# Attention with a learned distance bias and a two-layer FFN: weights' low bits on ScalarE, more first-layer rows on VectorE, new ranks for the early work

## The chip, the cores and the metric

The kernel runs on one core of one Trainium2 chip. The metric is the device time of one execution in microseconds; before the change the median of three runs is 672.18 us (670.63 to 674.49). A core has TensorE (PE; matmuls, with the loading of weights beside it, PEld), VectorE (DVE), ScalarE (ACT), GpSimd (POOL) and SyncE (SP), which here only issues DMAs. Each engine works through its own queue in order; a wait holds everything behind it on that engine.

## The reference

Attention over 4 batches, 8 heads, 576 positions and a head dimension of 64, with a bias that a small network makes from the distance of two positions, and then a feed-forward block over all 2304 tokens. All inputs are 32-bit floats except the two FFN weights, which are 64-bit floats.

```python
scores = scale * np.matmul(q, k.transpose(0, 1, 3, 2))
rel = (pos[:, None] - pos[None, :]).astype(np.float32)
x = (np.log1p(np.abs(rel)) / np.log1p(np.maximum(pos[:, None], 1.0)))[..., None]
bias = np.maximum(x @ w1 + b1, 0.0) @ w2        # 32 hidden units, 8 heads
scores = scores + bias.transpose(2, 0, 1)[None]
attn = softmax(scores);  attn_out = attn @ v
h = attn_out_tokens @ w_in                      # 512 -> 2048
g = h * np.clip(h + 3.0, 0.0, 6.0) / 6.0
out = g @ w_out                                 # 2048 -> 512
```

## The kernel before

**Bias tables.** The bias depends on the batch in nothing, so it is made once, in 36 groups of 16 query rows each. `z_group` (L854 to 871) makes the first layer: four tiles of [128, up to 576] for each group, each a maximum of a distance table `T` against a column (on VectorE, L865) or a Relu with a bias column (on ScalarE, L869). Which engine makes which of the four is read from a pattern of letters by `zeng`: A is ScalarE, D is VectorE; `z0` holds for groups 0 to 11, `z1` for 12 to 15, `zeng` for 16 to 35 (far groups, of which only the distances up to the farthest are made). `bias_mm` and `bias_far` multiply with `w2_sb` on TensorE (L907, L886) into one of three two-bank PSUM tiles, `bias_out` empties them on ScalarE (L925), and `bias_store` sends the block to DRAM (L939, on ScalarE's DMA queue). A correction column `cv_sb` for each distinct pattern is copied at the start (L1105). `load_bias` brings tables back from DRAM tile by tile (L500, on SyncE's queue), after all rows that the tile needs were stored.

**Attention.** 144 tiles of 128 query rows. For each: QK on TensorE (L536 is a warm-up product, L539 and L559 the scores), sum with the bias and row maximum on VectorE (L571), exponent on ScalarE (L582). The first 32 tiles (batches 0 and 1, first half of the rows) are `direct`: transposed on TensorE (L634), brought to SBUF on ScalarE (L637), multiplied with V in 32-bit (L675, L686). The others are split into a high and a low 16-bit part (L129 on ScalarE, L146 on VectorE) and transposed by DMA (L654).

**Weights.** `w_in` and `w_out` come as 64-bit floats, in eight pieces of 1 MB each (128 rows of 1024 numbers), and are read as pairs of 32-bit words. `f64_load` (L248) loads a piece, w_in into one of two buffers `w`, w_out into parts of the `wo` and `z_e` tiles. `f64_abs` takes the high word: ScalarE writes its absolute value, scaled, as a 32-bit float (L258), and GpSimd multiplies the high word by zero in place, which leaves its sign bit (L259). `f64_pack` then makes the 32-bit float on VectorE in three passes: clamp with a row maximum (L266), shift left by three and OR the sign (L269), and OR the three top bits of the low word (L272). A row's power-of-two scale follows, and `split_w` makes the high 16-bit part (L129) and the low one (L146): mode A does them on ScalarE and VectorE, mode R scales in place on GpSimd (L134), takes the high part on ScalarE and the low one on GpSimd (L139). `wm1` and `wm2` are the modes for the eight pieces of each weight. `w_in` is staged in `wo`, so w_out's loads into `wo` wait until w_in is split.

**FFN.** `ffn` is a generator with a step for each of 16 slices of hidden units (12 matmuls, L790, then L780, L773, L767, L769) and for parts of the output (L813, L823). Its first run is opened at tile 21 (`START`), when w_in is ready; w_out must be ready before its second layer. `open_steady` at tile 37 writes what is left of it, and from there TensorE's order is fixed as written.

**What sets the order.** The kernel is written as one long program; a scheduler gives every instruction a rank in the order of writing, simulates time, and lets each engine take the ready instruction of lowest rank. `ahead(k)` writes what is in its block with a rank k lower; `low(gen, key)` writes a generator's steps with a rank higher by the configured number (1000 for both weights). Pacing numbers say how many steps of each generator are written for each tile: `rw1` for w_in, `rf0` for the first FFN, `rf` for later ones. `behind(k)` makes a load wait at issue for the k-th bias load.

Of the kernel before, what the change touches and what calls it, by code (L numbers as in the profile page):

```python
# [13 lines left out]
U32 = mybir.dt.uint32  # L14
AF = mybir.ActivationFunctionType
# [4 lines left out]
D = 64  # L20
# [7 lines left out]
CQ = 2.0 ** -25  # L28
VC = 5 * 128
CFG = {'z0': 'AD', 'gz': 12, 'z1': 'AD', 'gz2': 16, 'zeng': 'DDA', 'sg': 'P', 'wm1': 'A', 'wm2': 'RRAAAAAA', 'hl': 'A', 'gl': 'PP', 'vm': 'A', 'g0': 8, 'rwi': 2.0, 'rw0': 0.3, 'rw1': 0.7, 'ro': 0.85, 'rb': 1.7, 'rf0': 1.3, 'rf': 2.0, 'rf1': 1.55, 'la': 6, 'gq': 2, 'gap': 0.0, 'wu': 8, 'act': 'o', 'g1': 2, 'w64': 5, 'rfo': 2.3, 'tv': 'A', 'pw': 1000, 'po': 1000, 'gr': 'AD', 'wb': 3, 'fb': 2, 'spn': 45, 'sw': 37, 'ws': 2, 'kn': 10, 'kw': 1, 'os': 10, 'ro2': 2.0, 'bo': 12, 'rb0': 1.5, 'psw': 21, 'xp': 0, 'mw': 2, 'he': 0}  # L30
# [5 lines left out]
def attention_moe_kernel(  # L36
# [214 lines left out]
    def f64_abs(t, u):  # L251
        if len(t.shape) == 3:
            tv, u = t.rearrange("p a (c w) -> p a c w", w=2), u.rearrange("p (a c) -> p a c", a=2)
            lo, hi = tv[:, :, :, 0], tv[:, :, :, 1].bitcast(F32)
        else:
            tv = t.rearrange("p (c w) -> p c w", w=2)
            lo, hi = tv[:, :, 0], tv[:, :, 1].bitcast(F32)
        nc.scalar.activation(out=u, in_=hi, func=AF.Abs, scale=F64_BIAS)  # L258
        nc.gpsimd.tensor_scalar(  # L259
            out=hi, in0=hi, scalar1=0.0, scalar2=1.0, op0=ALU.mult, op1=ALU.mult  # L260
        )
        return lo, hi.bitcast(U32), u

    def f64_pack(lo, sign, u, top, first=0.0):
        ub = u.bitcast(U32)
        nc.vector.tensor_scalar(  # L266
            out=u, in0=u, scalar1=F64_MAX, scalar2=first, op0=ALU.min, op1=ALU.max, accum_out=top,
        )
        nc.vector.scalar_tensor_tensor(  # L269
            out=ub, in0=ub, scalar=3, in1=sign, op0=ALU.logical_shift_left, op1=ALU.bitwise_or  # L270
        )
        nc.vector.scalar_tensor_tensor(  # L272
            out=ub, in0=lo, scalar=29, in1=ub, op0=ALU.logical_shift_right, op1=ALU.bitwise_or
        )
# [9 lines left out]
    def w_in_prep():  # L284
# [15 lines left out]
        def sign(k, t):  # L300
            c, fs = at(k)
            return f64_abs(t, stage[:, c, fs])
# [26 lines left out]
    def w_out_prep():  # L329
# [19 lines left out]
        def sign(k, t):  # L349
            if k % 2:  # L350
                u = const.tile([128, 2 * S], F32, tag="kb1", name="cu")
            else:
                u = pools["e"].tile([128, 2 * S], F32, tag="cu", name="cu")
            u = u[:, 0:1024]
            return (*f64_abs(t, u), u)
# [672 lines left out]
    def aux(n):  # L1028
# [25 lines left out]
        if b + 1 < B and t < 4 and p >= 1:  # L1054
            if b + 1 not in vgen:
                vgen[b + 1] = v_scale(b + 1)
# [18 lines left out]
    nc.sync.dma_start(out=bp, in_=psi)  # L1075
# [4 lines left out]
    nc.vector.memset(cv_sb, 0.0)  # L1080
# [18 lines left out]
    for k in range(4):  # L1099
        nc.tensor.matmul(out=cps[32 * k:32 * k + 32, 0:1], lhsT=w2_sb, rhs=b1_sb)  # L1100
    for c, pat in enumerate(pats):
        for k in range(4):
            if pat[k]:
# [30 lines left out]

    gen_b = repeat(bias_step)
    gen_w = low(w_in_prep(), "pw")
    gen_v = v_scale(0)
# [5 lines left out]
    HOLD, LAST = 2, NT + 5  # L1143
# [35 lines left out]
    def open_steady():  # L1179
        nonlocal phase  # L1180
        for k in count():
# [3 lines left out]
            if k % 2 and emitted[3] < NG:  # L1185
# [17 lines left out]
    def ffn_step():  # L1203
        nonlocal phase
        taken[0] += 1
        r = next(queue[0], "end")
# [16 lines left out]
    for n in range(-1, NT + 7):  # L1223
# [5 lines left out]
        if n == 12:  # L1229
# [91 lines left out]
```

## Time and profile before

| | before |
|---|---|
| median of three runs | 672.18 us (670.63 to 674.49) |
| the profiled execution | time 673.99 us, span 672.2 us |
| TensorE busy | 634.2 us, 94% of the span |
| weight loads (PEld) | 452.4 us, 67% |
| ScalarE busy | 506.4 us, 75% |
| VectorE busy | 460.0 us, 68% |
| GpSimd busy | 207.6 us, 31% |
| DMA | 130.57 MB, mean 194 GB/s |
| mean granted TensorE clock | 0.977 |

The span runs from the first to the last instruction; the time of an execution is that and what lies around it. A busy share is a mean over stages with different limits. The granted clock is given in parts of TensorE's full speed. A wait names the instruction that stood and the one that came last before it could go.

### The profile page before, as it was taken

How to read it: one execution, taken by the hardware profiler on the slowest of the kernel's cores; microseconds unless marked ns; L12 is line 12 of the kernel's file. 1: busy time of each engine (PE TensorE's matmuls, PEld its weight loads, DVE VectorE, ACT ScalarE, POOL GpSimd, SP SyncE). 2: the span in 40 equal slices, each digit the busy share in tenths (PEclk: the TensorE clock that was granted, in tenths of full speed). 3: DMA queues.
4: the chain of work that ended last, by engine and by line, in shares of the span. 5: the costliest groups of instructions: out<-in, count | busy, mean ns of one | idle time of the engine just before them, and what ended most of it. 6: DMA issues, size and time to landing. Idle time of an engine off the chain costs nothing. (4 is left out here: it accounts for less than half of the span.)

```text
span 672.2 us, 14784 instructions
## 1 busy us (share of the span) xinstructions
PE 634.2 (94%) x5424; PEld 452.4 (67%) x5424; DVE 460.0 (68%) x1114; ACT 506.4 (75%) x1000; POOL 207.6 (31%) x267
## 2 busy tenths in 40 slices
PE   7666799897999999999999999999999999999997
PEld 3223455575676667788888887777777777777775
DVE  6898858999846887677678768776677667720310
ACT  7986677888967998999689879876798669822620
POOL 0212124666111441145034414531245215300420
PEclk9987899898899999999999999999999999999999
DMA  8888966654496999999999999899878986530000
GB/s 293 287 328 310 362 240 236 245 190 166 107 214 187 269 189 237 256 229 208 260 269 253 216 219 202 187 164 184 210 144 167 194 179 124 110 74 20 1 11 29
DMA packets 176648, 130.57 MB, mean 194 GB/s; under 512 B 138304, under 2 KB 145728, under 8 KB 175552
## 3 DMA queue, kind: packets, MB, share of 16 engines
q1 hardware_dynamic: 166784, 114.14, 70.3%
q10 hardware_dynamic: 9792, 15.49, 7.3%
q8 instruction: 42, 0.69, 0.5%
q14 instruction: 30, 0.25, 0.1%
HBM read 77.54 MB, written 15.49 MB: 138 GB/s over the span
## 5 line engine op out<-in xcount | busy, mean ns | idle before, releaser
L790 PE MATMUL h_ps<-x,wi 128*128 128x256 f16 (+1 forms) x1536 | 200.0, 288 | 2.2 <-DVE p_v L161 1.0
L813 PE MATMUL o_ps<-g,wo 128*128 128x256 f16 (+1 forms) x1536 | 196.0, 286 | 0.0
L790 PEld LDWEIGHTS <-wi 128*128 128x128 f16 x1536 | 147.9, 98 | 50.4 <-issue 11.8
L813 PEld LDWEIGHTS <-wo 128*128 128x128 f16 x1536 | 146.9, 98 | 46.9 <-issue 8.8
L769 POOL TENSOR_TENSOR g<-t,g 128x256 f16<-128x256 f32 (+1 forms) x128 | 100.8, 797 | 187.5 <-ACT g L767 186.7
L582 ACT ACTIVATE bt<-bt,sm 128x576 f32<-128x576 f32 x144 | 110.7, 769 | 43.1 <-DVE sm L571 41.4
L146 DVE SCALAR_TENSOR_TENSOR hl<-bt,sm,hl 128x576 f16<-128x576 f32 x112 | 93.9, 851 | 25.5 <-ACT hl L129 22.2
L129 ACT ACTIVATE hl<-bt,sm 128x576 f16<-128x576 f32 x112 | 84.2, 766 | 3.4 <-ACT bt L582 2.3
L773 DVE SCALAR_TENSOR_TENSOR t<-t,t,h_ps 128x320 f32<-128x320 f32 (+1 forms) x112 | 57.0, 515 | 41.7 <-ACT t L780 40.8
L418 POOL TENSOR_TENSOR qkl<-st,qkh 128x576 fp32r<-128x576 f32 (+2 forms) x48 | 54.8, 1163 | 67.7 <-ACT qkh L411 67.0
L767 ACT ACTIVATE g<-t 128x256 f16<-128x256 f32 (+1 forms) x128 | 55.3, 439 | 21.3 <-DVE t L773 21.1
L571 DVE CUSTOM_DVE_ANT_0 bt<-s_ps,bt 128x576 f32<-128x576 f32 x88 | 65.1, 750 | 8.0 <-PE s_ps L559 4.5
L780 ACT ACTIVATE t<-h_ps,t,hr 128x320 f32<-128x320 f32 (+1 forms) x112 | 64.2, 585 | 5.2 <-PE h_ps L790 4.3
L823 ACT ACTIVATE ot<-o_ps,os 128x256 f32<-128x256 f32 (+1 forms) x32 | 15.8, 492 | 45.5 <-PE o_ps L813 45.5
L590 DVE TENSOR_SCALAR sm<-sm 128x1 f32<-128x1 f32 x112 | 16.8, 151 | 40.7 <-ACT bt L582 40.6
L925 ACT ACTIVATE bo<-b_ps,cv_sb,isc 128x576 f32<-128x576 f32 (+36 forms) x60 | 35.9, 640 | 4.0 <-PE b_ps L886 2.1
L865 DVE TENSOR_SCALAR z_e<-T,nbp 128x576 f32<-128x576 f32 (+17 forms) x69 | 31.4, 500 | 7.7 <-PE b_ps L886 6.6
L634 PE MATMUL t_ps<-eye_sb,bt 128*128 128x128 f32 x160 | 26.2, 298 | 10.5 <-DVE sm L571 8.1
L571 DVE CUSTOM_DVE_ANT_0 bt<-s_ps,k 128x576 f32<-128x576 f32 x40 | 28.7, 752 | 9.6 <-PE s_ps L559 7.6
L869 ACT ACTIVATE z_e<-T,bp 128x576 f32<-128x576 f32 (+17 forms) x43 | 29.0, 698 | 8.1 <-PE b_ps L886 4.6
L634 PEld LDWEIGHTS t_ps<-eye_sb,bt 128*128 128x128 f32 x160 | 18.6, 150 | 21.9 <-DVE sm L571 10.7
L721 PE MATMUL pv_ps<-at,vh 128*64 128x320 f16 (+1 forms) x432 | 32.0, 293 | 0.0
(128 smaller groups left out, 835.9 us busy)
## 6 DMA issues: line engine op xcount, KB each, us to landing
bt<-bias SPq DMA_DIRECT2D x36, 576.0 KB, 5.8
w<-in_w_in_dram SPq DMA_DIRECT2D x8, 1024.0 KB, 7.9
vs<-in_vp_dram SPq DMA_DIRECT2D x24, 320.0 KB, 4.8
st<-in_qk_dram SPq DMA_DIRECT2D x16, 448.0 KB, 4.3
bias<-bo ACTq DMA_DIRECT2D x20, 295.5 KB, 5.3
wo<-in_w_out_dram SPq DMA_DIRECT2D x5, 1024.0 KB, 6.2
bias<-bo ACTq DMA_DIRECT2D x16, 288.0 KB, 6.9
bt<-bias SPq DMA_DIRECT2D x32, 144.0 KB, 3.3
```

The lines of the kernel that those rows point to most:

```text
L129: nc.scalar.activation(out=out, in_=full, func=AF.Copy, scale=scale)
L146: nc.vector.scalar_tensor_tensor(out=out, in0=full, scalar=scale, in1=high, op0=ALU.mult, op1=ALU.subtract)
L418: nc.gpsimd.tensor_sub(out=lo[:, c:c + w], in0=t[:, c:c + w], in1=hi[:, c:c + w].bitcast(F32))
L571: nc.vector.tensor_tensor_reduce(out=halves(bt), in0=ps, in1=halves(src), op0=ALU.add, op1=ALU.min, scale=-0.125, scalar=3.0e38, accum_out ...
L582: nc.scalar.activation(out=bt, in_=bt, func=AF.Exp, scale=-1.0, bias=sm[:, 0:1], accum_out=total)
L634: nc.tensor.transpose(tp[:, 128 * c:128 * c + 128], bt[:, j:j + 128], eye_sb)
L767: nc.scalar.activation(out=g[:, 0], in_=uu, func=AF.Copy)
L769: e.tensor_sub(out=g[:, 1], in0=uu, in1=g[:, 0])
L773: nc.vector.scalar_tensor_tensor(out=t_t[f], in0=t_t[f], scalar=cols(f)[2], in1=h_t.pop(f)[:, 0:n], op0=ALU.min, op1=ALU.mult,)
L780: nc.scalar.activation(out=t_t[f], in_=h_t[f][:, 0:n], func=AF.Relu, scale=cols(f)[0], bias=cols(f)[1],)
L790: nc.tensor.matmul(out=h_t[f][:, 0:n], lhsT=wi[:, a, c, f * 128:(f + 1) * 128], rhs=x[:, e, c], start=(k == 0), stop=(k == 3 * KC - 1),)
L813: nc.tensor.matmul(out=ops[:, 0:n], lhsT=wo[:, a, f, e * 128:(e + 1) * 128], rhs=g_t[f][:, r], start=(f == 0 and a == 0 and r == 0), stop= ...
```

## The change

`f64_abs` gets a third step: it reads the low word's upper 16 bits as an unsigned integer, multiplies by 7.499 / 65535 and writes the result, 0 to 7, as a 16-bit integer into the lower half of the high word, which GpSimd has cleared but for the sign. The mode decides on which engine; both weights have mode A, ScalarE, for all pieces. With that the third pass of `f64_pack` is left out, since the OR of the sign brings the three bits along.

The patterns change: `z0` from AD to ADD, `zeng` from DDA to ADDD. `wm1` goes from A for all pieces to R for the first, `wm2` from R for the first two to R for the first. Pacing: `rw1` 0.7 to 0.6, `rf0` 1.3 to 1.6, `rf` 2.0 to 1.95, `wb` 3 to 8. Every function that writes work is wrapped by `ranked`, which moves its rank until the steady part begins; of the new ranks seven are not zero: `a_z` 300, `a_bo` -1000, `a_vl` -15, `a_st` -15, `a_wp` -40, `a_ld` -100, `a_wl` -300. V's scales are wrapped by `low` with 0. The load of psi moves to ScalarE's queue (`s2`). The other new keys (`tn`, `s1`, `il`, `dn`, `v1`, `hold`) have values that leave the code as it was.

```diff
+LOW3 = 7.499 / 65535
...
-'z0': 'AD', 'zeng': 'DDA', 'wm1': 'A', 'wm2': 'RRAAAAAA', 'rw1': 0.7, 'rf0': 1.3, 'rf': 2.0, 'wb': 3
+'z0': 'ADD', 'zeng': 'ADDD', 'wm1': 'RAAAAAAA', 'wm2': 'RAAAAAAA', 'rw1': 0.6, 'rf0': 1.6, 'rf': 1.95, 'wb': 8
+'a_z': 300, 'a_bo': -1000, 'a_vl': -15, 'a_st': -15, 'a_wp': -40, 'a_ld': -100, 'a_wl': -300, 'l31': 'A', 'l32': 'A', 's2': 1
...
-    def f64_abs(t, u):
+    def f64_abs(t, u, mode):
         if len(t.shape) == 3:
...
+            t16 = t.bitcast(U16).rearrange("p a (c w) -> p a c w", w=4)
+            top16, low16 = t16[:, :, :, 1], t16[:, :, :, 2]
...
         nc.scalar.activation(out=u, in_=hi, func=AF.Abs, scale=F64_BIAS)
         nc.gpsimd.tensor_scalar(
             out=hi, in0=hi, scalar1=0.0, scalar2=1.0, op0=ALU.mult, op1=ALU.mult
         )
-        return lo, hi.bitcast(U32), u
+        if mode == "P":
+            nc.gpsimd.tensor_scalar(
+                out=low16, in0=top16, scalar1=LOW3, scalar2=1.0, op0=ALU.mult, op1=ALU.mult
+            )
+        elif mode == "A":
+            nc.scalar.activation(out=low16, in_=top16, func=AF.Copy, scale=LOW3)
+        return lo if mode == "D" else None, hi.bitcast(U32), u
...
         nc.vector.scalar_tensor_tensor(
             out=ub, in0=ub, scalar=3, in1=sign, op0=ALU.logical_shift_left, op1=ALU.bitwise_or
         )
+        if lo is None:
+            return
         nc.vector.scalar_tensor_tensor(
             out=ub, in0=lo, scalar=29, in1=ub, op0=ALU.logical_shift_right, op1=ALU.bitwise_or
         )
...
-    nc.sync.dma_start(out=bp, in_=psi)
+    (nc.scalar if cfg['s2'] else nc.sync).dma_start(out=bp, in_=psi)
...
+    def ranked(f, key):
+        def g(*a):
+            with ahead(0 if steady[0] else cfg[key]):
+                return f(*a)
+        return g
...
+    z_group = ranked(z_group, "a_z")
...
+    bias_out = ranked(bias_out, "a_bo")
+    bias_store = ranked(bias_store, "a_st")
...
+    load_v = ranked(load_v, "a_vl")
+    load_direct = ranked(load_direct, "a_ld")
+    load_qk = ranked(load_qk, "a_ld")
...
+    f64_load = ranked(f64_load, "a_wl")
...
+    f64_pack = ranked(f64_pack, "a_wp")
...
-    gen_v = v_scale(0)
+    gen_v = low(v_scale(0), "a_v")
```

## Rows read from the trace of the kernel before

**Rows 1.** The page's 40 slices, busy tenths of TensorE (a slice is 16.8 us).

```profile
PE   7666799897999999999999999999999999999997
```

**Rows 2.** Busy us by stretch: PE, PEld, DVE, ACT, POOL, granted clock, DMA share, GB/s.

```profile
5.00:34.00 29.00, 21.39 (x207) 9.06 (x206) 23.50 (x53) 27.73 (x39) 4.06 (x3) 1.00 0.89 325
34.00:84.00 50.00, 35.55 (x204) 17.76 (x204) 45.84 (x95) 35.53 (x58) 7.80 (x7) 0.84 0.90 333
84.00:118.00 34.00, 32.23 (x235) 19.43 (x233) 24.69 (x60) 25.72 (x48) 11.68 (x10) 0.98 0.65 240
118.00:168.00 50.00, 43.78 (x329) 30.41 (x327) 47.48 (x100) 42.64 (x83) 31.04 (x29) 0.92 0.56 198
168.00:290.00 122.00, 119.54 (x1120) 86.99 (x1119) 88.13 (x234) 105.36 (x215) 28.24 (x37) 0.98 0.92 212
```

**Rows 3.** Waits between 5 and 50 us: us in total, times, longest.

```profile
PE s_ps L536 <- ACT bo L925: 4.9, 1, 4.9
PE b_ps L907 <- ACT z_a L869: 2.4, 4, 1.3
```

**Rows 4.** The same view between 50 and 84 us, then between 118 and 175 us.

```profile
PE t_ps L634 <- DVE sm L571: 4.9, 3, 2.4
...
PE t_ps L634 <- DVE sm L571: 2.2, 1, 2.2
```

**Rows 5.** Timeline of TensorE, two PV products of one form.

```profile
79.75 4.73 PE L675 MATMUL pv_ps<-atf,vf 128*64 128x256 f32 x20
...
85.98 2.53 PE L675 MATMUL pv_ps<-atf,vf 128*64 128x256 f32 x20
```

**Rows 6.** The same windows of line L272 alone: VectorE busy us and count, clock, DMA.

```profile
5.00:34.00 29.00, 2.43 (x2) 1.00 0.89 325
34.00:84.00 50.00, 7.51 (x6) 0.84 0.90 333
84.00:118.00 34.00, 2.92 (x2) 0.98 0.65 240
118.00:168.00 50.00, 8.51 (x6) 0.92 0.56 198
```

**Rows 7.** Instructions by line and form, 0 to 168 us: busy us, mean ns.

```profile
L146 DVE SCALAR_TENSOR_TENSOR wi<-wo,w1s,wi 128x1024 f16<-128x1024 f32 x8 | 10.1, 1275 | 0.1
L139 POOL TENSOR_TENSOR wo<-cu,wo 128x1024 f16<-128x1024 f32 x2 | 4.7, 2338 | 1.3 <-DMA wo<-in_w_out_dram 1.3
L865 DVE TENSOR_SCALAR z_a<-T,nbp 128x576 f32<-128x576 f32 x16 | 7.6, 512 | 1.5 <-PE b_ps L907 1.5
L129 ACT ACTIVATE wo<-cu 128x1024 f16<-128x1024 f32 x2 | 2.1, 1058 | 2.7 <-POOL cu L134 2.7
```

**Rows 8.** Timeline of ScalarE: start us, us, instruction.

```profile
6.50 1.43 ACT L869 ACTIVATE z_a<-T,bp 128x576 f32<-128x576 f32 x2
...
117.66 1.06 ACT L129 ACTIVATE wo<-cu 128x1024 f16<-128x1024 f32 x1 [2.39 <-POOL cu L134]
118.62 0.55 ACT L780 ACTIVATE t<-h_ps,c,hs 128x256 f32<-128x256 f32 x1
```

**Rows 9.** What SyncE's DMA queue waited for, 0 to 180 us.

```profile
SPq L248 <- DVE wo L272: 32.3, 5, 15.8
SPq L248 <- DVE cu L272: 23.3, 5, 9.3
```

**Rows 10.** The last of these windows for line L869 alone: ScalarE busy us and count.

```profile
168.00:290.00 122.00, 17.13 (x27) 0.98 0.92 212
```

**Rows 11.** Timeline of ScalarE, the first-layer rows at the start.

```profile
5.16 1.44 ACT L869 ACTIVATE z_e<-T,bp 128x576 f32<-128x576 f32 x2 [3.15 <-DVE bp L1089]
```

**Rows 12.** Timeline of ScalarE and TensorE around 37 us.

```profile
32.77 2.17 ACT L129 ACTIVATE wi<-wo,w1s 128x1024 f16<-128x1024 f32 x2
...
37.04 1.15 PE L536 MATMUL s_ps<-T,eye_sb 128*128 128x288 f32 x2 [4.91 <-ACT bo L925]
```

**Rows 13.** Timeline of VectorE, the first attention tile's softmax.

```profile
39.68 0.76 DVE L571 CUSTOM_DVE_ANT_0 bt<-s_ps,bt 128x576 f32<-128x576 f32 x1
```

More of the change, by code (lines that the diff above doesn't have):

```diff
@@ L14 @@
 U32 = mybir.dt.uint32
+U16 = mybir.dt.uint16
 AF = mybir.ActivationFunctionType
@@ L301, in sign @@
             c, fs = at(k)
-            return f64_abs(t, stage[:, c, fs])
+            return f64_abs(t, stage[:, c, fs], pick("l31", k))
         def pack(k, tu):
@@ L354, in sign @@
             u = u[:, 0:1024]
-            return (*f64_abs(t, u), u)
+            return (*f64_abs(t, u, pick("l32", k)), u)
         def pack(k, tu):
@@ L631, in soft_low @@
             tp = s_bank("t_ps").rearrange("p a b -> p (a b)")
+            if n < cfg["tn"]:
+                for _ in range(cfg["tw"]):
+                    nc.tensor.matmul(out=tp[:, 0:128], lhsT=eye_sb, rhs=eye_sb)
             for c in range(5):
@@ L1053, in aux @@
                 split_v_b(*units[k])
-        if b + 1 < B and t < 4 and p >= 1:
+        if b + 1 < B and t < 4 and p >= 1 and n >= cfg["v1"]:
             if b + 1 not in vgen:
-                vgen[b + 1] = v_scale(b + 1)
+                vgen[b + 1] = low(v_scale(b + 1), "a_v")
             next(vgen[b + 1], None)
@@ L1079, in attention_moe_kernel @@
     nc.sync.dma_start(out=T[:, 0:512], in_=ltab[:, 0:512])
-    nc.vector.memset(cv_sb, 0.0)
+    if cfg["s1"]:
+        nc.gpsimd.memset(cv_sb, 0.0)
+        for c, pat in enumerate(pats):
+            for k in range(4):
+                if pat[k]:
+                    nc.gpsimd.memset(cv_sb[32 * k:32 * k + 32, c:c + 1], 1.0)
+    else:
+        nc.vector.memset(cv_sb, 0.0)
     nc.vector.memset(c36[:, 0:1], 3.0 * CQ)
@@ L1100, in attention_moe_kernel @@
         nc.tensor.matmul(out=cps[32 * k:32 * k + 32, 0:1], lhsT=w2_sb, rhs=b1_sb)
+    if cfg["s1"]:
+        nc.vector.tensor_scalar(
+            out=cv_sb, in0=cv_sb, scalar1=cps[:, 0:1], scalar2=None, op0=ALU.mult
+        )
     for c, pat in enumerate(pats):
         for k in range(4):
-            if pat[k]:
+            if pat[k] and not cfg["s1"]:
                 rows = slice(32 * k, 32 * k + 32)
@@ L1142, in attention_moe_kernel @@
     START, SWITCH = 21, cfg["sw"]
-    HOLD, LAST = 2, NT + 5
+    HOLD, LAST = cfg['hold'], NT + 5
     in_order = ctx.enter_context(ExitStack())
@@ L1184, in open_steady @@
             ffn_step()
-            if k % 2 and emitted[3] < NG:
+            if k % cfg['il'] and emitted[3] < NG:
                 bias_step()
@@ L1205, in ffn_step @@
         taken[0] += 1
-        r = next(queue[0], "end")
+        with ahead(0 if steady[0] else cfg["a_ff"]):
+            r = next(queue[0], "end")
         if r == "w2":
@@ L1228, in attention_moe_kernel @@
             next(gen_v, None)
-        if n == 12:
+        if n == cfg["dn"]:
             distances()
```

19 lines of the change are left out of this document (18 added, 1 removed).

## The prediction

> **What bounds the kernel now.** I read the page's 40 slices first [rows 1]. From about the twelfth slice on TensorE is in the highest tenth to the end, with one dip; the room lies in the first ten slices, with 6 to 9 tenths. So nothing that the change does to ScalarE or VectorE late in the span can pay much, and what it does before 168 us pays only where TensorE stands still there. I then cut the early part by what runs in it [rows 2] and subtract TensorE's busy time from each stretch: idle are 29.0 - 21.4 = 7.6 us from 5 to 34 us (call it A), 50.0 - 35.6 = 14.4 us from 34 to 84 us (B), 1.8 us from 84 to 118 us (C), 6.2 us from 118 to 168 us (D), and 2.5 us of the 122 us after that (E). About 30 us are to be had before 168 us, and no more, unless the clock rises too.
>
> Who is full in each stretch differs, and that is what the change must be held against. In A ScalarE works 27.7 of 29.0 us; VectorE 23.5. In B VectorE works 45.8 of 50 us and ScalarE 35.5, while the DMA engines are 0.90 busy. In C nobody is full but TensorE. In D VectorE works 47.5 of 50 us and ScalarE 42.6. In E ScalarE is at 105.4 of 122. The waits say the same: up to 50 us TensorE waits for ScalarE (4.9 us once for a bank that a bias row block had to leave, 2.4 us for first-layer rows) [rows 3]; after that for VectorE's softmax (4.9 us in B, 2.2 us in D) [rows 4]. The granted clock is 0.84 in B and 0.92 in D [rows 2], so between the levels of 1.2 and 2.4 GHz part of the time: one and the same product of 20 matmuls takes 4.73 us just after a thin stretch and 2.53 us a few us later [rows 5].
>
> **Part 1, the low bits.** Sixteen weight pieces (eight of w_in, eight of w_out) lose their last VectorE pass, L272: two in A with 2.4 us, six in B with 7.5, two in C with 2.9, six in D with 8.5, together 21.3 us [rows 6]. In their place ScalarE runs 16 copies of 128x1024, 16-bit in and out, with steps of four elements. No row shows such a copy. The nearest is the 128x1024 copy with a constant scale: 1.06 us long [rows 7], 0.96 us from its start to that of the next instruction [rows 8]. Below, it could not go under what a ScalarE instruction of 1024 elements takes at all here, so 0.96; above I take the slowest mean of the L272 it replaces, 2.92 / 2 = 1.46 us in C [rows 6]. I use 0.96, the row with the same engine, operation and size: 15.4 us in all, up to 23 at the upper end. So 21 us leave VectorE and 15 go to ScalarE.
>
> The Trainium skill, "ScalarE: Activation LUTs", section "Rules for kernel authors", says the opposite of what is done here: a multiplication belongs on VectorE rather than on ScalarE. The rows above have the two passes nearly equal, because the VectorE one reads two 32-bit operands; going by the rule one would book no gain for this part, and the sum below would end near the time of before. That case stands among the rivals.
>
> The pass also sits in a chain: ScalarE's absolute value, GpSimd's clearing of the high word, the new copy, then VectorE's shift-and-or, which until now waited for GpSimd alone. In return the last reader of a w_in buffer, and with it what the next weight load waits for, is no longer L272. SyncE's queue now stands 32.3 us in five waits and 23.3 us in five more for exactly that instruction [rows 9], and everything behind it in that queue (bias and value loads) stands too. One pass leaves that chain and one of about the same length enters: I cost the release at nothing, with one pass of 1 to 1.5 us for each of the three dependent rounds of w_in loads either way as its bounds, so plus or minus 5 us.
>
> **Part 2, first-layer rows.** In the first twelve groups VectorE makes two rows of three instead of one of two: 32 instead of 24, so ScalarE loses 8. Two ScalarE rows take 1.43 us back to back [rows 8], so 8 x 0.72 = 5.7 us less there, and 8 x 0.51 = 4.1 us more on VectorE [rows 7], which has 5.5 us idle in A [rows 2] and loses two L272 there. In the far groups (20, all in E) ScalarE makes 20 rows instead of 27. The 27 take 17.1 us [rows 10], so the 7 some 4.4 us of ScalarE, but TensorE is idle for only 2.5 us of E, and other releasers share that: I take 0.5 us. Three more copies of one column for the additional patterns of rows lie on VectorE at the start, beside its idle time in A.
>
> **Part 3, piece modes.** The first w_in piece gets its low half on GpSimd instead of VectorE (1.28 us less there), the second w_out piece gets it on VectorE instead of GpSimd (1.28 us more, and 2.34 us plus a scaling pass less on GpSimd) [rows 7]. GpSimd is busy for 4.1 of 29 us in A and 7.8 of 50 in B [rows 2], so it hides the first; C has 9.3 us of VectorE idle to hide the second.
>
> **Part 4, ranks, pacing and loads.** The psi load goes to ScalarE's queue, one slot of SyncE earlier for all that follows it. ScalarE's first row waits 3.15 us for the product of that load [rows 11]; one slot is about 0.4 us. The first-layer rows go 300 ranks ahead, the emptying of the bias banks 1000 behind, weight loads 300 and the pack 40 behind, and the third w_out load waits for a later bias load. All of this moves work and adds none. Its price depends on the order that the scheduler writes, which no row shows; it is bounded by the idle time it can fill or open, and I give it -6 to +10 us, and zero in the sum, except that it lets A's relief come through.
>
> **The sum, stretch by stretch.** A: ScalarE, which is full, loses 5.7 us and gains two copies, 1.9 us: -3.8, of which I count 3.5. B: VectorE falls by six L272, 7.5 us, and one low half of 1.28, from 45.8 to 37.0 us; ScalarE rises by 5.8 to 41.3. The fuller of the two falls by 4.5 us; transfers limit part of this stretch (0.90 busy), so I count 3. C: 0. D: VectorE falls by six L272, 8.5 us, to 39.0; ScalarE rises by 5.8 to 48.4 of 50, above the 47.5 that VectorE had. The fuller engine has 0.9 us more: +1. E: -0.5. Start: -0.4. Together -3.5 - 3 + 1 - 0.5 - 0.4 = -6.4 us. The span of the profiled execution is 672.2 us, its own time 673.99, the median of three runs 672.18; the difference of span and time is 1.8 us and stays, and the median is 1.8 us below the profiled execution. So I take 672.2 - 6.4, near **666 us** for the median.
>
> **Rivals.**
> *ScalarE becomes what VectorE was.* For: over A to D the busier engine has 23.5 + 45.8 + 24.7 + 47.5 = 141.5 us (VectorE) now, and afterwards 27.7 + 35.5 + 25.7 + 42.6 = 131.5 plus 15.4 minus 5.7 = 141.2 us (ScalarE). If a queue that full is what makes tiles late, whichever engine it is, nothing is won; only start and E remain, and the time is 671 us, with 669 to 675 about it. Against: B and A have different full engines, and the change relieves each in its place. This is also where the rule of the Trainium skill above would lead.
>
> *Late bank emptying, slower.* L925, which empties the bias banks, loses 1000 ranks, while the weight passes on the same in-order queue, now one more for each piece, do not. The pattern is in the trace: two weight copies hold ScalarE for 2.17 us from 32.77 us on, and TensorE's next score matmul, at 37.04, has waited 4.91 us for an emptying behind them [rows 12]. Several w_in pieces are worked on while the 16 near groups run. If two or three more of them cut in like that, at up to 4.9 us each, the tables and with them all softmaxes come 10 to 15 us later, and A's relief of 3.5 is gone: 672 + 10 to 15 - 3 = 679 to 684, say 680 us. It decides from the point where the eighth group's store lands later than now, since the first tile's bias load waits for it. Against: rows cannot run far ahead, as only two groups' buffers and three banks exist.
>
> *More than the sum.* The early gap of B closes further, the clock stays up (2.2 us for one product alone [rows 5]), and tiles start earlier by all of A: up to half of the 30 us idle, 655 us. It is the far end of the forecast, not a case of its own.
>
> **How the numbers follow.** A measurement of this kernel can tell about 0.5%, 3.4 us, from no change. Forecast with its far end (655 to 668.5 us): 0.58. ScalarE in VectorE's place (669 to 675): 0.22. Late emptying or another order that stalls (over 675.5): 0.20. The likeliest case's own range is 657 to 669. To leave out no more than 2 in 10, the range goes from 655 to 679: it cuts off gains of over half the idle time and the far half of the slower case, and takes in the copy's upper price (16 x 0.5 = 8 us of ScalarE) and the bounds of the release.
>
> **What would show it.** Right: no L272; a 16-bit ScalarE copy near 1.0 us at 16 places; VectorE under 40 of 50 us in B; the first softmax before 39.68 us [rows 13]; SyncE's waits for L272 replaced by shorter ones; the start of TensorE's full stretch some 6 us earlier. Wrong: the copy at 1.5 us or more; first softmax after 40 us with TensorE waiting for L925; ScalarE over 48 of 50 us from B on with the softmax exponent late; or a full stretch that begins earlier and a tail that gives it back.

## The result and the profile after

| | before | after |
|---|---|---|
| median | 671.96 us (4 runs, 670.63 to 674.49) | 679.27 us (4 runs, 678.25 to 680.08) |
| ratio | | 1.0103, 95% interval 1.007 to 1.0136 |
| the profiled execution | 673.99 us, span 672.2 | 678.25 us, span 676.4 |
| TensorE busy; rest of the span | 634.2; 38.0 us | 633.5; 42.9 us |
| ScalarE busy, VectorE busy | 506.4, 460.0 us | 531.9, 452.1 us |

The change made the kernel 7.3 us slower, where 6.2 us faster was forecast. TensorE's busy time is nearly the same; the span holds 4.9 us more in which it does nothing. First, busy time by stretch after the change, with the columns and stretches of [rows 2]:

```profile
5.00:34.00 29.00, 22.06 (x207) 10.54 (x206) 24.08 (x60) 27.14 (x33) 5.94 (x4) 0.88 0.84 304
34.00:84.00 50.00, 34.95 (x206) 17.11 (x208) 40.34 (x83) 47.11 (x62) 8.67 (x7) 0.83 0.86 308
84.00:118.00 34.00, 28.42 (x189) 15.90 (x189) 21.52 (x65) 29.10 (x48) 8.69 (x8) 0.90 0.66 238
118.00:168.00 50.00, 43.90 (x333) 30.81 (x330) 40.06 (x92) 48.67 (x76) 24.16 (x24) 0.93 0.59 218
168.00:290.00 122.00, 117.89 (x1109) 84.84 (x1110) 94.25 (x236) 104.42 (x215) 30.99 (x41) 0.99 0.86 208
```

The fuller engine has changed sides. From 34 to 84 us ScalarE now works 47.1 of 50 us (35.5 before) and VectorE 40.3 (45.8); from 118 to 168 us ScalarE is at 48.7. From 84 to 118 us, where nobody but TensorE had been full, TensorE lost 3.8 us of work (32.2 to 28.4). What fills ScalarE is seen when the same view is asked for the new copy, L273, alone (ScalarE busy us and count); [rows 6] had VectorE's pass:

```profile
5.00:34.00 29.00, 4.98 (x2) 0.88 0.84 304
34.00:84.00 50.00, 14.96 (x6) 0.83 0.86 308
84.00:118.00 34.00, 5.10 (x3) 0.90 0.66 238
118.00:168.00 50.00, 14.19 (x6) 0.93 0.59 218
```

39.2 us up to 168 us and another 0.5 behind it, for sixteen copies (two lie across a border), or 2.48 us for one; I had booked 0.96. The row of the line itself (shortest, median and longest in ns):

```profile
L273 ACT ACTIVATE w<-w x8: 2472/2494/2509, 22.2 to 79.6; 128x1024 uint16<-128x1024 uint16 x8
```

Next, the waits of the new kernel between 5 and 50, 50 and 84, and 84 and 118 us (us in total, times, longest), to be held against [rows 3, 4]:

```profile
PE b_ps L924 <- ACT bo L942: 10.8, 4, 5.8
PE s_ps L550 <- ACT bo L942: 2.9, 1, 2.9
...
PE s_ps L550 <- ACT atf L654: 5.3, 3, 2.9
...
PE s_ps L553 <- ACT atf L654: 4.6, 3, 3.7
```

Up to 118 us TensorE's waits for VectorE's softmax [rows 4] have mostly given way to waits for ScalarE: for L942, which empties the bias banks (L925 before), and for L654, which brings the transposed exponents to SBUF. For the emptying it is 10.8 + 2.9 = 13.7 us before 50 us; the kernel before has the 4.9 us of [rows 3] and this row, 6.8 us together:

```profile
PE b_ps L907 <- ACT bo L925: 1.9, 1, 1.9
```

ScalarE's and TensorE's timelines, at one place of each kind, say why:

```profile
22.22 2.47 ACT L273 ACTIVATE w<-w 128x1024 uint16<-128x1024 uint16 x1
24.45 1.49 ACT L942 ACTIVATE bo<-b_ps,cv_sb,isc 128x576 f32<-128x576 f32 x2
...
25.27 2.15 PE L924 MATMUL b_ps<-z_e,w_sb 128*32 128x288 f32 x16 [5.82 <-ACT bo L942]
...
99.72 4.78 ACT L273 ACTIVATE wo<-wo 128x1024 uint16<-128x1024 uint16 x2
104.22 0.81 ACT L654 ACTIVATE atf<-t_ps 128x640 f32<-128x640 f32 x1
...
105.09 1.33 PE L553 MATMUL s_ps<-qk 64*128 64x288 f32 x4 [3.68 <-ACT atf L654]
```

Both waits end with an instruction that stood behind L273 in ScalarE's queue. Two copies back to back hold it for 104.22 - 99.72 = 4.50 us, 2.25 us for each. And the first softmax, the row that answers to [rows 13], has not come earlier; it waited for its bias load:

```profile
40.52 0.76 DVE L585 CUSTOM_DVE_ANT_0 bt<-s_ps,bt 128x576 f32<-128x576 f32 x1 [1.86 <-DMA bt<-bias]
```

SyncE's waits for the last VectorE pass of a piece, 55.6 us in [rows 9], have shrunk as forecast:

```profile
SPq L250 <- DVE cu L281: 13.4, 3, 6.6
...
SPq L250 <- DVE wo L281: 7.3, 3, 4.0
```

But other waits took their place: all waits of weight loads in this view, whatever ended them, come to 65.5 us (L250), against 66.3 before (L248). The last w_in piece is split at 89.2 us (89.8 before), so nothing was won with it.

### The profile page after: what moved, and what is told of

It is laid out like the page before. It is cut to its first block, busy times and chain, and to the rows that moved or that the text cites. A ratio compares the mean times of both kernels' runs of the same rounds, so it can differ in the third digit from the quotient of the medians.

```text
span 676.4 us, 14781 instructions
## 1 busy us (share of the span) xinstructions
PE 633.5 (94%) x5424; PEld 452.5 (67%) x5424; DVE 452.1 (67%) x1116; ACT 531.9 (79%) x1001; POOL 205.7 (30%) x267
## 4 chain that ended last, share of the span: by engine, by line
PE 77%; ACT 10%; DMA 5%; DVE 4%; issue 3%; SPq 0%; POOL 0%; ACTq 0%; DVEq 0%
PE o_ps L830 28%; PE h_ps L807 26%; PE s_ps L573 9%; PE pv_ps L738 7%; PE b_ps L903 2%; PE pv_ps L692 2%; DMA va<-in_vp_dram 2%; ACT bt L596 2%; ACT w L273 1%; DVE z_e L882 1%; DMA bias<-bo 1%; ACT wo L273 1%; DMA wo<-in_w_out_dram 1%; PE b_ps L924 1%; DMA vf<-in_vp_dram 1%
## 5 line engine op out<-in xcount | busy, mean ns | idle before, releaser
L786 POOL TENSOR_TENSOR g<-t,g 128x256 f16<-128x256 f32 (+1 forms) x128 | 102.7, 813 | 171.1 <-ACT g L784 160.3
L148 DVE SCALAR_TENSOR_TENSOR hl<-bt,sm,hl 128x576 f16<-128x576 f32 x112 | 92.7, 844 | 25.1 <-ACT hl L131 23.0
L131 ACT ACTIVATE hl<-bt,sm 128x576 f16<-128x576 f32 x112 | 83.8, 767 | 6.6 <-ACT bt L596 2.8
L790 DVE SCALAR_TENSOR_TENSOR t<-t,t,h_ps 128x320 f32<-128x320 f32 (+1 forms) x112 | 56.8, 515 | 42.7 <-ACT t L797 40.5
L432 POOL TENSOR_TENSOR qkl<-st,qkh 128x576 fp32r<-128x576 f32 (+2 forms) x48 | 53.9, 1143 | 86.1 <-ACT qkh L425 84.1
L882 DVE TENSOR_SCALAR z_e<-T,nbp 128x576 f32<-128x576 f32 (+17 forms) x80 | 39.6, 548 | 5.5 <-PE b_ps L903 4.3
L942 ACT ACTIVATE bo<-b_ps,cv_sb,isc 128x576 f32<-128x576 f32 (+36 forms) x60 | 35.6, 634 | 4.0 <-DMA bias<-bo 2.6
L553 PE MATMUL s_ps<-qk 64*128 64x288 f32 x128 | 26.8, 498 | 6.3 <-ACT atf L654 4.8
L886 ACT ACTIVATE z_e<-T,bp 128x576 f32<-128x576 f32 (+17 forms) x32 | 21.9, 696 | 8.7 <-PE b_ps L903 4.5
L573 PE MATMUL s_ps<-qkh 64*128 64x288 f32 x192 | 27.2, 344 | 1.5 <-ACT atf L654 1.5
```

Source lines behind the costliest of these rows:

```text
L131: nc.scalar.activation(out=out, in_=full, func=AF.Copy, scale=scale)
L148: nc.vector.scalar_tensor_tensor(out=out, in0=full, scalar=scale, in1=high, op0=ALU.mult, op1=ALU.subtract)
L573: nc.tensor.matmul(out=s_t[n + j][:, a, 0:HALF], lhsT=w[q], rhs=m[rows, cs], start=(k == 0), stop=(k == 2),)
L786: e.tensor_sub(out=g[:, 1], in0=uu, in1=g[:, 0])
L790: nc.vector.scalar_tensor_tensor(out=t_t[f], in0=t_t[f], scalar=cols(f)[2], in1=h_t.pop(f)[:, 0:n], op0=ALU.min, op1=ALU.mult,)
```

## The experiments

Theory: the price of the copy, 2.49 us where 0.96 was booked, makes the loss. Rivals: the new order (ranks, pacing, patterns) loses by itself; ScalarE is the wrong engine for the pass at any price. Letters as in the prediction: A is 5 to 34 us, B to 84, C to 118, D to 168.

### The price by itself

The kernel before, with nine kinds of 128x1024 copies on ScalarE, written behind the last work.

```diff
+    pairs = [(q(s16, 4), q(d16, 4)), (q(s16, 4), d16[:, 0:1024]), ... ]
+    for src, dst in pairs:
+        for _ in range(2):
+            nc.scalar.activation(out=dst, in_=src, func=AF.Copy, scale=0.5)
```

> The kernel before, with nine forms of ScalarE copies of 128x1024 hung on behind its last product, two of each: 16-bit in and out at steps of four, each side dense instead, both dense, 32-bit at steps of two, a 16-bit float at steps of four, 16-bit out at steps of two. If the written side is what costs, dense out takes 1.0 to 1.2 us and stepped out 2.5; if the read side, the reverse; if each side adds, 1.7 with one side stepped. If it is the 16-bit integer as such, the dense one takes 2.5 too. The span grows by the sum, some 30 us, and says nothing else.

One execution. The copies ran beside TensorE's last products, from 640 us on, and not behind them, so the span grew by 4 us and not by 30; that says nothing of their lengths. ScalarE's timeline. The four rows are: 16-bit, read and written in steps of four; two with the step on the reading side only; dense on both sides; 16-bit floats in steps of four.

```profile
640.18 2.49 ACT L1333 ACTIVATE wi<-wi 128x1024 uint16<-128x1024 uint16 x1
...
645.97 2.28 ACT L1333 ACTIVATE wi<-wi 128x1024 uint16<-128x1024 uint16 x2
...
653.47 1.04 ACT L1333 ACTIVATE wi<-wi 128x1024 uint16<-128x1024 uint16 x1
...
660.59 2.49 ACT L1333 ACTIVATE wi<-wi 128x1024 f16<-128x1024 f16 x1
```

It is the write. A stepped read costs a tenth of a microsecond (2.28 / 2 = 1.14 against 1.04), the stepped 16-bit write 1.45 us, whether integer or float (with the step on the writing side alone it is 2.49 us too). Other kinds in the same run: 16-bit written in steps of two 1.35 us, whole 32-bit words in steps of two 1.14. The Trainium skill, "ScalarE: Activation LUTs", section "What ACT_TABLE_LOAD costs", gives 186 ns and 0.833 ns for each element with immediate scale and bias, for 32-bit and 16-bit numbers alike, which makes 1.04 us; the dense row agrees, and the narrow stepped write takes 2.4 times as long, so there the measurement decides.

### The parts one by one

Each is the kernel before with one part of the change.

```diff
only_low_act: -l31 'D', l32 'D'             +l31 'A', l32 'A'
pat:          -z0 'AD', zeng 'DDA'          +z0 'ADD', zeng 'ADDD'
rank:         -a_z 0, a_bo 0, ...           +the seven ranks of the change
pace:         -rw1 .7, rf0 1.3, rf 2, wb 3  +rw1 .6, rf0 1.6, rf 1.95, wb 8
modes:        -wm1 'A', wm2 'RRAAAAAA', s2 0 +wm1 'RAAAAAAA', wm2 'RAAAAAAA', s2 1
```

The pass alone on ScalarE:

> The kernel before with the 16-bit pass on ScalarE alone: old patterns, ranks, pacing, modes. Theory 1: slower than before by 6 to 15 us, 678 to 687, with copies of 2.5 us. Theory 2: within 3 us of before, 669 to 675.

697.36 us, 1.0386 (1.0347 to 1.0425): 25 us lost, above both expected ranges and more than three times what the whole change loses. In the old order the pass is the dear part; with the rest of the change beside it most of that loss is gone, though no other part gains anything alone, as the next runs show.

The patterns alone:

> The kernel before with the new patterns of first-layer rows alone. By the sum of the prediction, 4 us faster, 666 to 669. If any change of the work makes the scheduler write a worse order: 674 to 682.

673.17 us against 673.29, 1.0005 (0.9979 to 1.0032). The first softmax comes at 37.9 us instead of 39.7, the 14th at 87.4 instead of 86.1: the lead is gone within B.

The ranks alone, and the pacing alone:

> The kernel before with the seven new ranks alone. If the ranks are good by themselves: 665 to 670; if they cost: 675 or more; booked in the prediction with 0 (-6 to +10).

> The kernel before with the four new pacing numbers alone. If the first FFN, written faster, leaves TensorE without work at the hand-over to the second layer: 675 or more. If pacing is neutral: 670 to 674.

677.41 us, 1.0066 (1.0032 to 1.0099), and 676.23 us, 1.0047 (1.0021 to 1.0073). Both are ahead at first (the 14th softmax at 81.3 and 82.6 us, before 86.1), and both lose it later: FFN's second layer begins at 175.3 and 175.2 us instead of 174.0.

The piece modes and the psi load alone:

> The kernel before with the piece modes of the change (first piece of w_in and only the first of w_out with scaling and low half on GpSimd) and the load of psi on ScalarE's queue; no pass moved, old ranks, old pacing, old patterns. My prediction booked this part at nothing and the load at -0.4 us: 670 to 674 us. Rival, that this part carries some of the loss: 675 us or more.

680.01 us, 1.0113 (1.007 to 1.0157). I missed this one: GpSimd does not hide the first low half. GpSimd's and VectorE's timelines:

```profile
34.13 4.38 POOL L141 TENSOR_TENSOR wi<-wo,wi 128x1024 f16<-128x1024 f32 x1 [0.79 <-ACT wi L131]
...
36.55 3.04 DVE L286 SCALAR_TENSOR_TENSOR wo<-w,wo 128x1024 uint32<-128x1024 uint32 x1
```

GpSimd's pass took 4.38 us instead of 2.34 [rows 7], and a VectorE pass beside it 3.04 instead of the 7.51 / 6 = 1.25 us that L272 (here L286) took in B before [rows 6]. But that is not where the 1.1% is lost: the first softmax comes at 39.6 us (39.7 before) and the 14th at 83.3, ahead of the 86.1 before. The loss arises behind them, up to the 32nd softmax (168.0 us against 158.2), while w_out is worked on; what in this part makes it was not separated. The parts do not add up: single, they lose 3.9, 0.1, 0.7, 0.5 and 1.1%; together 1.0%.

### The pass taken away from ScalarE again

```diff
low_dve:  -'l31': 'A', 'l32': 'A'  +'l31': 'D', 'l32': 'D'
low_pool: -'l31': 'A', 'l32': 'A'  +'l31': 'P', 'l32': 'P'
```

The changed kernel with the pass on VectorE:

> The changed kernel, but the low bits are again OR'd by VectorE (its third pass, as before); patterns, ranks, pacing and piece modes stay as changed. Theory 1 (the 16-bit copy on ScalarE costs 2.5 us instead of the 0.96 that was booked, and fills ScalarE's queue): the time falls from 679 to 672 or lower, 666 to 673. Theory 2 (late emptying of the bias banks, from the ranks): it stays at 676 or more.

679.26 us, 1.0127 (1.0077 to 1.0177), no better than the change: a miss of theory 1, which had 673 at most. But the way there is another. The first softmax comes at 35.97 us, 3.7 us before [rows 13]: so much do patterns, ranks, pacing and modes bring together in A when no copies take it back (alone, the patterns bring 1.7 and the ranks 2.0). It goes again at the hand-over to the FFN's second layer. Between 160 and 200 us TensorE's waits have this row:

```profile
PE t_ps L651 <- DVE sm L585: 10.0, 2, 5.9
```

and the windows show what it costs from 168 to 200 us (TensorE's busy time comes first; the kernel before has 32.00 of 32 us at a clock of 0.91 there):

```profile
168.00:200.00 32.00, 27.84 (x202) 19.05 (x202) 20.59 (x60) 20.02 (x37) 3.78 (x4) 0.76 0.68 189
```

TensorE's order has two transposes of late tiles ahead of the second layer, and both wait for VectorE, which has its passes back. This spoke against the price theory until the order was held fixed, below.

The changed kernel with the pass on GpSimd:

> The changed kernel, but GpSimd makes the 16-bit pass instead of ScalarE; everything else as changed. Theory 1: ScalarE is relieved of 16 x 2.5 = 40 us and VectorE keeps its 21 us less, so it is the fastest of this call, 660 to 670. If GpSimd's pass is as slow as ScalarE's or the chain through GpSimd is what counts, 672 to 678. Theory 2: 676 or more.

682.70 us, 1.0167 (1.0136 to 1.0197), the slowest of the changed kernel's variants so far, where theory 1 had it the fastest. GpSimd pays the same for the stepped write (median 2.50 us), and VectorE's low half of w_in beside it took 1.80 us on average, against 1.28 [rows 7].

### Ranks and pacing in the new order

```diff
bo_rank0:  after    -'a_bo': -1000  +'a_bo': 0
dve_az0:   low_dve  -'a_z': 300     +'a_z': 0
dve_rank0: low_dve  -all seven      +0
dve_pace:  low_dve  -the new pacing +the old
```

> The changed kernel with the rank of the emptying of the bias banks at 0 instead of 1000 behind. Theory 2: the time falls by 4 us or more, to 675 or lower, and TensorE's waits for the emptying before 50 us fall from 10.8 to under 5 us. Theory 1: within 2 us of 679, 677 to 681.

677.93 us, 1.0111 (1.0073 to 1.0148), beside 1.0103 for the change. The order of TensorE, VectorE and SyncE is that of the changed kernel, and ScalarE's differs in two places. TensorE's waits for the emptying before 50 us stay (10.0 us at L924, against 10.8). The 1000 ranks that I had feared do next to nothing.

> The changed kernel with the low bits on VectorE and the first-layer rows at rank 0 instead of 300 ahead. If the far rows, put ahead of w_out's last scale on VectorE, make the hand-over to the second layer late: 674 or less (679 with the rank). If the pacing does it: 677 to 681.

677.97 us, 1.0086 (1.0056 to 1.0115). Not one instruction stands elsewhere than in low_dve; 1.0086 and 1.0127 are two measurements of one order, which shows how far two such numbers can differ.

> The changed kernel with the low bits on VectorE and all new ranks at 0. If ranks cost the 7 us: 674 or less, and near 668 if the rows moved to VectorE pay as forecast. If the pacing does: 677 to 681.

> The changed kernel with the low bits on VectorE and the four pacing numbers of before (rw1 0.7, rf0 1.3, rf 2.0, wb 3). If the first FFN, written at 1.6 steps for each tile, runs out before w_out is ready and leaves TensorE empty at the hand-over: 674 or less. If the ranks do it: 677 to 681.

681.93 us, 1.0132 (1.007 to 1.0195), and 676.45 us, 1.006 (1.003 to 1.009). The ranks, taken away, win nothing back. The old pacing gives 1.006 against the 1.0086 of dve_az0, a smaller step than the one between the two measurements of one order, so a cost of the new pacing is not shown here.

### A denser write

A write in steps of two costs 1.35 us. For w_in the sign words can go densely to the place where the split weights will stand:

```diff
-            nc.gpsimd.tensor_scalar(out=hi, in0=hi, ...)
-            nc.scalar.activation(out=low16, in_=top16, func=AF.Copy, scale=LOW3)
+            nc.gpsimd.tensor_scalar(out=sg, in0=hi, ...)
+            nc.scalar.activation(out=sl, in_=top16, func=AF.Copy, scale=LOW3)
```

In the changed kernel (dense_wi), and in the kernel before with w_out's pass left on VectorE (old_dense_wi):

> The changed kernel, but for the eight w_in pieces GpSimd writes the sign words densely into w_in's own, still unused place, so that ScalarE's 16-bit copy writes every second 16-bit word (1.35 us by the run on prices) instead of every fourth (2.49). If the price of the copy is what was mis-sized: ScalarE has 8 x 1.14 = 9 us less before 90 us and the time falls by 3 to 8 us, to 671 to 676. If the new order is what costs: 677 to 681.

> The kernel before, with the pass on ScalarE for the eight pieces of w_in alone, where the sign words go to a buffer of their own, so that the copy writes every second 16-bit number and not every fourth (1.35 us in the run that measured prices, against 2.49). w_out's eight pieces keep the pass on VectorE, and patterns, ranks and pacing are the old ones. Theory 'the price of the copy, and a configuration that was fitted to it': 668 to 674 us, since VectorE loses 8 passes in the stretch where it is full and ScalarE gains 11 us where it has room. Rival 'ScalarE's queue is the wrong place for it': 678 us or more.

683.28 us, 1.0179 (1.0117 to 1.0241), and 680.96 us, 1.0131 (1.0078 to 1.0184): misses. The copies cost what they should (the row is from old_dense_wi; dense_wi has a median of 1346 ns):

```profile
L270 ACT ACTIVATE wi<-w x8: 1347/1354/1392, 19.8 to 68.1; 128x1024 uint16<-128x1024 uint16 x8
```

But the order that the scheduler wrote is another, and the 14th softmax came at 87.7 and 95.5 us. These two say nothing for or against the price, since price and order changed together.

### The price alone, in an unchanged order

So I changed one operand. The copy writes the whole high word, which is the cheap kind of write, and the weights' signs are lost. What each instruction waits for stays as it was, and in the two traces the instructions of VectorE, ScalarE and GpSimd stand in the same order, TensorE's too but for products that start together.

```diff
-            nc.scalar.activation(out=low16, in_=top16, func=AF.Copy, scale=LOW3)
+            nc.scalar.activation(out=hi.bitcast(U32), in_=top16, func=AF.Copy, scale=LOW3)
```

> The changed kernel with one operand altered: the copy on ScalarE writes a whole 32-bit word, the high word, and no longer every fourth 16-bit number (so the weights' signs are lost). The instructions of TensorE, VectorE, ScalarE and SyncE stand in the same order as in the changed kernel, row for row. In the run that measured prices a copy of this kind took 1.13 us, the changed kernel's 2.49. Theory 'the price of the copy': 16 copies shed about 1.3 us each, 21 us of ScalarE, and with my prediction's own sum the time comes to 664 to 671 us, 8 to 15 us under the changed kernel. Rival 'the new order' (ranks, pacing and patterns lose by themselves): 676 us or more.

666.92 us, 0.9907 (0.9876 to 0.9939): 12.4 us under the changed kernel, and faster than before. Busy time by stretch:

```profile
5.00:34.00 29.00, 20.89 (x206) 8.93 (x206) 26.84 (x61) 26.08 (x34) 6.04 (x5) 0.88 0.84 307
34.00:84.00 50.00, 38.68 (x235) 19.60 (x236) 42.80 (x94) 44.04 (x69) 8.28 (x7) 0.86 0.91 331
84.00:118.00 34.00, 30.20 (x217) 18.49 (x216) 22.50 (x63) 28.46 (x52) 9.31 (x9) 1.00 0.79 289
118.00:168.00 50.00, 47.25 (x373) 33.63 (x372) 45.94 (x113) 48.02 (x89) 26.84 (x27) 0.97 0.49 178
```

The wait that the changed kernel had at 105 us, in the same place of the same order:

```profile
96.66 2.20 ACT L273 ACTIVATE wo<-wo 128x1024 uint32<-128x1024 uint16 x2
98.72 0.72 ACT L654 ACTIVATE atf<-t_ps 128x640 f32<-128x640 f32 x1
...
99.49 0.76 PE L553 MATMUL s_ps<-qk 64*128 64x288 f32 x4 [1.15 <-ACT atf L654]
```

Two copies hold the queue for 2.06 us instead of 4.50, TensorE waits 1.15 instead of 3.68 us, and runs the same four products in 0.76 instead of 1.33 us. Between 5 and 50 us TensorE's waits for bank emptying fall too, from 13.7 to 7.8 us:

```profile
PE b_ps L924 <- ACT bo L942: 6.3, 3, 4.7
...
PE s_ps L550 <- ACT bo L942: 1.5, 1, 1.5
```

The starts of some instructions in the traces, in us, and how the span divides:

| | before | after | cheap_hi | low_dve | sign_half_wp0 |
|---|---|---|---|---|---|
| 1st softmax | 39.7 | 40.5 | 40.4 | 36.0 | 43.7 |
| 14th softmax | 86.1 | 87.3 | 82.4 | 83.8 | 85.6 |
| 32nd softmax | 158.2 | 166.0 | 154.9 | 155.4 | 165.8 |
| first product of FFN's second layer | 174.0 | 177.0 | 163.0 | 178.2 | 177.3 |
| span | 672.2 | 676.4 | 668.3 | 675.3 | 677.4 |
| TensorE busy | 634.2 | 633.5 | 630.7 | 631.8 | 631.7 |
| rest of the span | 38.0 | 42.9 | 37.6 | 43.5 | 45.7 |

At the same order the copy's price moves the 32nd softmax by 11.1 us and the second layer by 14.0; 8.1 us of that are left at the end of the two spans. The lead at the 14th softmax, 4.9 us, is there before the first FFN product, so the lost signs cannot have made it. Nor do products with the lost signs run faster: from 290 to 480 us, at a granted clock of 1.00 in both, the changed kernel and cheap_hi have these rows (busy us, mean ns):

```profile
L807 PE MATMUL h_ps<-x,wi 128*128 128x256 f16 x372 | 42.7, 273 | 0.0
...
L807 PE MATMUL h_ps<-x,wi 128*128 128x256 f16 x308 | 35.5, 273 | 0.0
```

The same in the old order:

> The kernel before with the pass on ScalarE and nothing else of the change, but with the copy that writes a whole 32-bit word (signs lost). Row for row the order of the run that put the pass alone on ScalarE (697.4 us). Theory 'the price of the copy': that run's loss of 25 us goes down to between -5 and +5 us against the kernel before, so 667 to 677 us. Rival 'ScalarE is the wrong engine for this pass at any price, since its queue holds the exponents and the emptying of banks': 685 us or more.

681.12 us, 1.0134 (1.0099 to 1.017), 16 us under the run with the dear copy, but not back at the kernel before: a miss by 4 us on the upper side, and under the rival's 685. A cheap copy on ScalarE pays with the change's order and loses with the old one. Both halves were needed, price and order; the price decides the sign of this change.

### A complete kernel with the narrow write on GpSimd

To have the cheap write on ScalarE and leave nothing out, the two small passes change roles.

```diff
+            nc.scalar.activation(out=lo, in_=top16, func=AF.Copy, scale=LOW3)
+            nc.gpsimd.tensor_scalar(out=sg, in0=hi, scalar1=0.0, scalar2=1.0, op0=ALU.mult, op1=ALU.mult)
+            return None, lo, u
```

Here `sg` is the low word's upper half as a 16-bit float. In the changed kernel (sign_half), and with the pack's rank at 0 instead of 40 behind (sign_half_wp0):

> The changed kernel, complete, with the two small passes the other way round: ScalarE writes the three low bits as a whole 32-bit number over the low word (the cheap kind of write, 1.13 us in the run that measured prices), and GpSimd then writes the sign into that word's upper half (the dear kind of write, about 2.5 us, on the engine that is busy for 12 to 50% of the stretches up to 168 us), so that VectorE still ORs one word. Everything else as in the changed kernel; but the scheduler writes another order, since GpSimd's pass now comes after ScalarE's. Theory 'the price of the copy on ScalarE': 664 to 672 us, at or below the kernel before, and well below the changed kernel's 679. Rival 'the chain' (GpSimd's 1.3 us more for each piece delay the pieces by as much as ScalarE gains): 675 to 680 us. A third, that the new order happens to stall: above 680 us.

> The last kernel (a complete one, with the wide write on ScalarE and the narrow one on GpSimd) with one rank changed: the pack goes 0 instead of 40 ranks ahead. With that the instructions of TensorE stand in the order of the changed kernel and of the one with the cheap copy up to the first slices of the FFN's second layer (8 groups of TensorE's rows differ, all at w_out; 17 of ScalarE's), where the last kernel's stood otherwise from the first bias banks on. Theory 'price of the copy, in the order that the change wrote': 666 to 671 us, under the kernel before by 0.2 to 0.9%, near the 666.9 of the kernel with the cheap copy. Rival 'the longer chain through GpSimd costs what ScalarE gains': 675 to 679 us, as the last kernel's 677.

677.36 us, 1.0078 (1.0053 to 1.0103), in the rival's range, and 680.08 us, 1.0113 (1.007 to 1.0156), above both ranges. The order is not the change's in either: in sign_half_wp0's trace TensorE's agrees with it up to 52 us, VectorE's only up to 24 us (a shift-and-or stands ahead of a clamp) and ScalarE's up to 20 us (the first copy stands ahead of first-layer rows). So price and order changed together here too, and these two runs do not test the price alone. Besides the order and the longer chain there is a third thing. Timelines of VectorE and GpSimd in sign_half_wp0:

```profile
33.96 2.75 POOL L272 TENSOR_SCALAR w<-w 128x1024 f16<-128x1024 f32 x1 [0.81 <-ACT w L271]
39.45 3.51 POOL L272 TENSOR_SCALAR w<-w 128x1024 f16<-128x1024 f32 x1 [2.74 <-ACT w L271]
...
34.25 3.26 DVE L148 SCALAR_TENSOR_TENSOR wi<-wo,w1s,wi 128x1024 f16<-128x1024 f32 x1
...
40.56 3.13 DVE L893 TENSOR_SCALAR z_a<-T,nbp 128x576 f32<-128x576 f32 x2
```

and VectorE's same work in cheap_hi:

```profile
32.83 1.27 DVE L148 SCALAR_TENSOR_TENSOR wi<-wo,w1s,wi 128x1024 f16<-128x1024 f32 x1
...
36.86 0.94 DVE L882 TENSOR_SCALAR z_a<-T,nbp 128x576 f32<-128x576 f32 x2
```

These VectorE instructions take 2.0 and 2.2 us longer beside GpSimd's pass. Five of the sixteen passes cost VectorE about 2 us each in that way; beside the others it lost 0.4 us at most, as with the clamp here, whose median is 1.21 us:

```profile
136.78 2.50 POOL L272 TENSOR_SCALAR wo<-wo 128x1024 f16<-128x1024 f32 x1
...
136.98 1.20 DVE L289 TENSOR_SCALAR_CACHE_REDUCE cu<-cu 128x1024 f32<-128x1024 f32 x1
```

So GpSimd's slack is paid for in part by VectorE: it works 44.9 us of B here, for 82 instructions, against 42.8 for 94 in cheap_hi. The Trainium skill, "SBUF — State Buffer", section "SBUF: two separate sides", says that VectorE and GpSimd share one pair of ports as an exclusive lock for a whole instruction, and that a VectorE instruction contends for it only in a two-port mode or, against a GpSimd instruction that reads SBUF, with two inputs in SBUF. L148, with two inputs, and the clamp, with one, agree; in what mode the first-layer rows (L893, one input) ran, no run shows. How much of the loss is chain, order or this was not separated. No version with all of the work beat the kernel before.

## Why the prediction was wrong

**The bounds (where TensorE stands still, and about 30 us to be had)** held. After the change the rest of the span grew by 4.9 us, and by the windows TensorE stands idle for 33.7 us from 5 to 168 us, against 30.0.

**Part 1, the copy: this step failed.** I booked 0.96 us, with 1.46 as the upper bound, because "the row with the same engine, operation and size" was the nearest. It wrote densely; the copy writes two bytes of every eight, and no row of before had that. Measured: 2.49 us long, 2.25 from start to start, outside the bounds. Sixteen of them are 36 us of ScalarE, not 15.4. With 2.25 in the prediction's own sum, A is -5.7 + 4.5 = -1.2; in B ScalarE comes to 35.5 + 13.5 = 49.0 against VectorE's 45.8, +3.2; in D to 42.6 + 13.5 = 56.1 against 47.5, +8.6; with -0.9 for E and the start that is +9.7 us. Measured: +7.3. With a cheap copy (1.14 us) in the same order the kernel takes 666.92 us: this run, and not the sum, shows that the mis-sized term makes the sign and nearly all of the size: 12.4 of the 13.3 us between forecast and measurement.

**The sum by the fuller engine fails too, stretch by stretch.** With the true price it has -1.2 us in A, +3.2 in B, 0 in C, +8.6 in D and -0.5 in E. TensorE's idle time, by the windows, changed by -0.7, +0.6, +3.8, -0.1 and +1.7 us. So the nearness of 9.7 to 7.3 is luck. In C ScalarE works 29.1 of 34 us and is not full, and yet TensorE waits there 3.68 us behind two copies; in D ScalarE is at 48.7 of 50 us and TensorE stands no longer than before.

**That cheap_hi comes out near the forecast 666 is luck as well.** A should have brought 3.5 us and brought nothing (first softmax 40.38 us): there a copy stands ahead of the bank emptying even when it is cheap. B gave TensorE 3.1 us more work (38.68 against 35.55), as forecast. D, booked at +1, gave 3.5 us more work (47.25 against 43.78) with ScalarE at 48.0 of 50 us. But TensorE's idle time grew by 2.0 us in C and by 4.0 in E, so that the rest of the span is 37.6 us, where the kernel before has 38.0. Of the 3.9 us between the two spans 3.5 lie in TensorE's busy time (630.7 against 634.2 us, at a mean granted clock of 0.98 in both). The forecast had all of its gain in idle time.

**The release of the w_in buffers at nothing** held: SyncE's waits for the last VectorE pass went from 55.6 to 20.7 us, those of all weight loads only from 66.3 to 65.5, and w_in was ready 0.6 us earlier.

**Part 2, the rows.** 5.7 us less ScalarE were booked in A; by themselves the patterns bring the first softmax 1.7 us earlier (37.9 against 39.7 us). That it would come through was wrong: the time is 1.0005 of before, and the lead is gone by the 14th softmax.

**Part 3 as hidden** was wrong. Alone, with the psi load, it loses 1.1%. The GpSimd pass slows a VectorE pass beside it (3.04 against 1.25 us), but the loss comes later, behind the 14th softmax. The psi load's 0.4 us did not come either: its issue now stands ahead of ScalarE's table load (1.17 us instead of 0.72), and ScalarE's first row begins at 5.22 us, against 5.16 [rows 11].

**Part 4 at nothing, -6 to +10 us,** held as a range: 4.1 us for the ranks alone (0.66%), 2.9 for the pacing alone (0.47%). In zero I had the middle of what was really a loss in the old order; with the copies on ScalarE, the same numbers belong to an order that wins once the copy is cheap.

**The rivals.** "ScalarE becomes what VectorE was" named the right place, ScalarE's queue, with too small a price (669 to 675 us). That a queue so full must make tiles late is refuted by cheap_hi: 48.0 of 50 us in D, and the tiles early. Which instruction stands in front of what decides, and for how long. "Late bank emptying" had the time (680) and the wait (5.8 us once; 13.7 in all before 50 us, against 6.8), but not the cause: without its 1000 ranks the order is nearly the same and the kernel takes 1.0111. The emptying is late behind copies of 2.47 us. Of what was to show the forecast wrong, "the copy at 1.5 us or more" and "first softmax after 40 us with TensorE waiting for L925" (now L942) both came.

**Open.** What in the modes, psi load included, costs 1.1% behind the 14th softmax. Why TensorE's idle time moved to C and E. And why the old order loses 1.3% with a cheap copy: the two orders differ in too many places to name one.

## What to carry to other kernels

Before an operation moves to another engine, look for a row with the same kind of write (width and step), not only the same engine, operation and size; where there is none, the upper bound has to reach far above the dense row, here to 2.4 times. A sum over the fuller engine of each stretch can come out near for the wrong reason: hold it against each stretch before trusting its total. An engine with idle time is not free if another stands while it works: five of sixteen GpSimd passes here cost VectorE about 2 us each. To tell a price from an order, change the price and leave every dependence as it is, so that the scheduler writes the same order; edits that only changed ranks, pacing or modes moved this kernel by 0.5 to 1.1%, and two measurements of one order lay 0.4% apart.

## What the hardware showed that was not expected

A 16-bit write in steps of eight bytes takes ScalarE 2.49 us for 128x1024, against 1.04 dense, 1.35 in steps of four bytes and 1.14 for whole 32-bit words in steps of eight; the reading side adds 0.1 us. GpSimd has the same price (median 2.50 us, against 1.17 for whole words in steps of eight). A VectorE pass with two inputs beside such a GpSimd pass ran 3.26 instead of 1.27 us, and two first-layer rows 3.13 instead of 0.94, while the clamp with one input kept its 1.2 us.
